# Linear attention and an expert layer on one core: where the routing counts, the turned key table and the first experts' products stand in the attention loop

## The chip, the cores and the metric

The kernel runs on one core of a Trainium2 chip. The metric is the device time of one execution in microseconds, on random inputs of fixed shape. A core has TensorE (PE, with its weight loads PEld), VectorE (DVE), ScalarE (ACT), GpSimd (POOL), and SyncE (SP), which issues most transfers. PE writes to PSUM, of which the kernel uses eight banks of 128 x 512 float32; DVE and ACT read it, POOL does not.

## The reference

Attention with random features for 8 batches of 8 heads, 576 tokens and 64 columns, and then a layer of 8 experts, of which each of the 4608 tokens takes one:

```python
def phi(x):
    proj = np.einsum('bhsd,md->bhsm', x, omega)
    sq = np.sum(x * x, axis=-1, keepdims=True) / 2.0
    h = proj - sq
    h = h - np.max(h, axis=-1, keepdims=True)
    return np.exp(h) / np.sqrt(m)
q_p, k_p = (phi(q_s), phi(k_s))                       # m = 128 features
kv = np.einsum('bhsm,bhsd->bhmd', k_p, v)
z = np.sum(k_p, axis=2)
num = np.einsum('bhsm,bhmd->bhsd', q_p, kv)
den = np.einsum('bhsm,bhm->bhs', q_p, z)[..., None] + 1e-06
...
x = num / den                                         # as (4608, 512)
logits = xn @ en.T / tau                              # of the normalized rows
expert_idx = np.argmax(logits, axis=1)
for e in range(E):
    mask = expert_idx == e
    h = np.maximum(x[mask] @ w1[e], 0.0)              # 512 to 1024 and back
    out[mask] = gate_w[mask, None] * (h @ w2[e])
```

## The kernel before, in words

**The attention loop** has 43 steps, `i` from 0 to 42, over 36 tiles of 128 tokens (4 pairs of batches, 9 tiles each; a batch ends in the middle of the fifth tile of its pair and at the end of the ninth). Steps 0 to 5 have keys only, steps 6 to 35 keys of tile `i` and queries of tile `i - 6`, steps 36 to 41 queries only; the last tile's numerators are in step 42. Keys and queries are projected (`proj`), DVE takes maxima, ACT the exponentials (`feats`). A step later the key features go into the batch's accumulators (`kvmm`, two banks, tags kv0 and kv1), and the query features are transposed into the two banks nu0 and nu1 (`qtr`), copied to SBUF as `qp` (`qcopy`, one half by ACT and one by DVE, in query-only steps both by ACT), and multiplied with the key table into the same two banks (`num`). DVE divides (`num_out`) and writes the token rows `xr` and the experts' logits by head, `lg`, which has one buffer.

**At a batch boundary** (steps 5, 9, 14, 18, 23, 27, 32, 36) ACT empties the accumulators into `kvs`. In the fifth tile of a pair the accumulations for both batches stand in one step. A step later the table is turned by four PE transposes into nu0 (`kv_turn`), DVE copies it out (`kv_turned`), and PE forms the logits' columns of the table behind the numerators (`kv_logits`), which DVE adds to `kvs` (`kv_logits_out`).

**Routing** (`routed`) runs in pieces for each group of three tiles: sum of the logits over heads and their maximum, selection `sel`, counts by PE (a triangular and three full matrices of ones, into nu1), positions, and for each tile an indirect store of its rows by POOL into the buffer `xs`, sorted by expert. Each `next(steps)` does a piece; the dictionaries `spare`, `mid`, `after` and `ends` say at which place of which step. All but the stores and three small copies a group is DVE's or PE's.

**First steps.** After the sixth group the fullest expert so far is picked. Its weights are loaded in steps 27 to 34 and split into high and low halves in steps 29 to 36 by ACT or DVE and POOL (`first_split`). Its first two tiles of rows are computed by `first_steps`, a generator of 38 pieces: two turn a tile of rows, most of the others are three products. A `next(fill)` does one piece. Behind the loop, the remaining pieces stand between the last group's routing, the table of steps that DVE builds, and its transpose `tp`.

**The expert part** then takes 36 steps of 128 rows with three products for one (high and low halves) and streamed weights.

The order on PE and POOL, in the loop also on DVE and ACT, is that of the code; a scheduler orders SP. In the loop of before:

```python
            late = (i,) in mid
            go(spare, i)
            if ts:
                qtr(iq - 1, 1 if late else 0)
            go(mid, i)
            if ts:
                qtr(iq - 1, 0 if late else 1)
            if i >= END - 1:
                next(fill)
```

## Time and profile before

| | |
|---|---|
| time, median of 3 runs | 701.2 us (700.13 to 702.5) |
| profiled execution, its time | 699.2 us |
| profiled execution, its span | 697.5 us |
| PE busy | 654.3 us (94%), 5977 instructions |
| PE weight loads busy | 543.8 us (78%) |
| DVE busy | 567.8 us (81%), 1127 instructions |
| ACT busy | 422.0 us (60%), 1081 instructions |
| POOL busy | 300.4 us (43%), 296 instructions |
| TensorE's granted clock, mean | 0.987 |

The span runs from the first to the last instruction of the profiled execution; the time is that of the whole execution and is a little longer. Busy shares are means over stages with different limits: the attention loop ends at about 249 us, the expert part takes the rest. A granted clock of 1.00 stands for 2.4 GHz, 0.50 for 1.2 GHz.

### The profile page before, as it was taken

The page shows a single profiled execution, that of the slowest core. Times are in us where ns is not written, and L with a number is a line of the kernel's source. Part 1 is how long each engine was busy: PE and PEld are TensorE (multiplying, and loading weights), DVE is VectorE, ACT ScalarE, POOL GpSimd, SP SyncE. Part 2 cuts the span into 40 slices and gives each one's busy share as a digit, 9 for nine tenths or more (in the row PEclk, how much of TensorE's full clock was granted, in tenths as well). Part 3 has the DMA queues.
Part 4 walks back from the last instruction along what each step waited for, and adds up shares of the span by engine and source line. Part 5 has one row for each costly group of instructions (what it writes and reads, how often), then busy time and mean ns, then how long its engine had stood idle before and what let it go on. Part 6 is the DMA issues. An engine that isn't in the chain of part 4 may idle for free. (4 is left out here: it accounts for less than half of the span.)

```text
span 697.5 us, 17954 instructions
## 1 busy us (share of the span) xinstructions
PE 654.3 (94%) x5977; PEld 543.8 (78%) x5978; DVE 567.8 (81%) x1127; ACT 422.0 (60%) x1081; POOL 300.4 (43%) x296
## 2 busy tenths in 40 slices
PE   6899999999796689999999999999999999999994
PEld 6788888888685578778778878788888888878872
DVE  3689899899796652668999999999989998999961
ACT  5798788788786632655374746465555655556430
POOL 2001222113645252444645555464645546463653
PEclk9999999999999979999999999999999999999997
DMA  6445665556942126767787777878688887878620
GB/s 220 142 147 173 181 189 184 185 185 230 333 157 92 63 97 230 237 196 199 209 238 187 223 199 211 200 224 215 199 217 210 224 200 220 200 223 221 178 94 30
DMA packets 142376, 131.85 MB, mean 189 GB/s; under 512 B 106758, under 2 KB 106886, under 8 KB 142288
## 3 DMA queue, kind: packets, MB, share of 16 engines
q1 hardware_dynamic: 135968, 110.30, 57.7%
q0 software_dynamic: 6320, 20.38, 7.7%
q8 instruction: 54, 0.88, 0.5%
q14 instruction: 34, 0.28, 0.1%
HBM read 83.78 MB, written 21.97 MB: 152 GB/s over the span
## 5 line engine op out<-in xcount | busy, mean ns | idle before, releaser
L208 POOL TENSOR_TENSOR w1l<-raww,w1h 128x1024 f32 x34 | 89.3, 2625 | 159.5 <-DVE w1h L207 159.5
L876 DVE COPY wd<-t 128x1024 uint16<-128x1024 uint16 x68 | 116.1, 1710 | 0.5 <-DMA t<-pl 0.5
L242 PE MATMUL nu<-w2h,hh 128*128 (+1 forms) x288 | 114.0, 396 | 0.7 <-POOL w2l L208 0.7
L242 PE MATMUL nu<-w2h,hl 128*128 (+1 forms) x288 | 113.8, 395 | 0.3 <-DVE hl L896 0.3
L242 PE MATMUL nu<-w2l,hh 128*128 (+1 forms) x288 | 113.6, 395 | 0.0
L242 PE MATMUL pa<-w1h,xl 128*128 (+1 forms) x280 | 110.9, 396 | 0.7 <-DVE xl L895 0.7
L242 PE MATMUL pa<-w1h,xh 128*128 (+1 forms) x280 | 110.9, 396 | 0.0
L242 PE MATMUL pa<-w1l,xh 128*128 (+1 forms) x280 | 110.6, 395 | 0.0
L892 ACT ACTIVATE hh<-wd 128x1024 fp32r<-128x1024 f32 x34 | 36.1, 1061 | 119.5 <-DVE wd L876 115.3
L475 POOL DMA_INDIRECT xs<-xr,posi x36 | 35.9, 998 | 138.6 <-DVE nmk L325 34.8
L332 ACT ACTIVATE ftk<-pjk,nmk 128x128 f32<-128x128 f32 x288 | 83.8, 410 | 15.5 <-DVE nmk L325 14.8
L321 PE MATMUL pjk<-om,kt 64*128 64x128 f32 x576 | 80.0, 298 | 6.5 <-DMA kt<-kT 6.3
L208 POOL TENSOR_TENSOR w2l<-raww,w2h 128x1024 f32 x34 | 82.6, 2430 | 0.7
L332 ACT ACTIVATE ftq<-pjq,nmq 128x128 f32<-128x128 f32 x288 | 79.8, 411 | 1.9 <-DVE nmq L325 1.8
L321 PEld LDWEIGHTS pjk<-om,kt 64*128 64x128 f32 x576 | 66.6, 199 | 14.1 <-issue 10.2
L321 PE MATMUL pjq<-om,qt 64*128 64x128 f32 x576 | 76.3, 285 | 0.8 <-ACT ftq L332 0.5
L242 PEld LDWEIGHTS nu<-w2h,hh 128*128 128x128 f32 x288 | 54.2, 188 | 14.0 <-POOL w2l L208 1.4
L321 PEld LDWEIGHTS pjq<-om,qt 64*128 64x128 f32 x576 | 63.6, 187 | 1.5 <-ACT ftq L332 0.7
L242 PEld LDWEIGHTS pa<-w1h,xl 128*128 128x128 f32 x280 | 52.6, 188 | 15.6 <-DVE xl L895 2.5
L242 PEld LDWEIGHTS nu<-w2h,hl 128*128 128x128 f32 x288 | 54.2, 188 | 13.6 <-DVE hl L896 0.7
L242 PEld LDWEIGHTS nu<-w2l,hh 128*128 128x128 f32 x288 | 54.2, 188 | 12.8
L242 PEld LDWEIGHTS pa<-w1l,xh 128*128 128x128 f32 x280 | 52.7, 188 | 12.3
(300 smaller groups left out, 1281.2 us busy)
## 6 DMA issues: line engine op xcount, KB each, us to landing
raww<-w1q SPq DMA_DIRECT2D x38, 512.0 KB, 4.4
raww<-w2q SPq DMA_DIRECT2D x38, 512.0 KB, 5.2
kt<-kT SPq DMA_DIRECT2D x36, 256.0 KB, 3.0
qt<-qT SPq DMA_DIRECT2D x36, 256.0 KB, 3.4
xgp<-xs SPq DMA_DIRECT2D x20, 260.5 KB, 3.1
xg<-xs SPq DMA_DIRECT2D x18, 260.5 KB, 3.1
rf<-w1q SPq DMA_DIRECT2D x4, 512.0 KB, 4.7
rf<-w2q SPq DMA_DIRECT2D x4, 512.0 KB, 5.6
```

The costliest lines, as they stand in the source:

```text
L208: il = nc.gpsimd.tensor_tensor(at(l, dp), raw, at(h, dp).bitcast(F32), op=ALU.subtract)
L242: done.append(nc.tensor.matmul(dst, x[:, c * P : (c + 1) * P], ws.rearrange("p o f -> p (o f)"), start=(begin and i == 0 and k == 0), stop ...
L321: nc.tensor.matmul(st["pj" + w, i, a][:, c, :], st[w, i][r, c, :], om[r, :], start=True, stop=True)
L332: nc.scalar.activation(ft[:, h, :], pj[:, h, :], AF.Exp, bias=nm[:, h : h + 1])
L475: w = nc.gpsimd.indirect_dma_start(out=xs, out_offset=bass.IndirectOffsetOnAxis(ap=posi, axis=0), in_=xr, in_offset=None, bounds_check=ROW ...
L876: nc.vector.tensor_copy(to, src)
L892: nc.scalar.activation(hh, wd[:, 0:F], AF.Relu)
```

## The change

It does six things. The table is turned into a bank with the accumulators' tag kv0. In the fifth tile of a pair the second accumulation stands a step later, for which key features have five buffers and values four (query features two and `qp` two). The counts are two sets of four products on half of the array's columns each, behind the numerators, and the transposes come in the order nu1, nu0. The copy of the turned table stands behind `qcopy`. In eleven of twelve groups the sums over heads and over experts, the masking of positions and their casts are POOL's. And `next(fill)` stands at other places: at the end of steps 37 and 38, behind the maxima in steps 39 to 42, and once more in step 42.

```diff
-                    vt = p1.tile([P, H, D + 1], F32, name=f"vt{i}{key}", tag="vt", bufs=3)
+                    vt = p1.tile([P, H, D + 1], F32, name=f"vt{i}{key}", tag="vt", bufs=4)
...
-            ft = p1.tile([P, 4, M], F32, name=f"ft{which}{i}_{a}", tag=f"ft{which}", bufs=3)
+            ft = p1.tile([P, 4, M], F32, name=f"ft{which}{i}_{a}", tag=f"ft{which}", bufs=5 if which == "k" else 2)
...
-            st["kvtr", sb, b] = tr = nu[0]
+            st["kvtr", sb, b] = tr = ps.tile([P, 512], F32, name=f"kvtr{sb}_{b}", tag="kv0")
...
-            st["qp", i, a] = qp = p1.tile([P, 4, P], F32, name=f"qp{i}_{a}", tag="qp", bufs=4)
+            st["qp", i, a] = qp = p1.tile([P, 4, P], F32, name=f"qp{i}_{a}", tag="qp", bufs=2)
...
         def routed(g):
 
+            eng = nc.gpsimd if g < NTILE // G - 1 else nc.vector
+
+            def total(out, x, axes):
+
+                if eng is nc.vector:
+                    eng.tensor_reduce(out, x.rearrange(axes), axis=AX.X, op=ALU.add)
+                    return
+                for n in (4, 2, 1):
+                    eng.tensor_tensor(x[:, :, 0:n] if n > 1 else out.unsqueeze(2), x[:, :, 0:n], x[:, :, n : 2 * n], op=ALU.add)
+
...
-            nc.vector.tensor_reduce(raw, st["lg", g].rearrange("p g h e -> p g e h"), axis=AX.X, op=ALU.add)
+            total(raw, st["lg", g], "p g h e -> p g e h")
+            if eng is nc.gpsimd:
+                yield
             mx = new("mx", [P, G])
...
-            yield
+            if eng is nc.vector:
+                yield
             sel = sels[g % 2][:, 0:G]
...
-            pr = nu[1][:, P : P + (G + 1) * E].rearrange("p (j e) -> p j e", e=E)
-            nc.tensor.matmul(pr, tri, sels[g % 2], start=True, stop=False)
-            for j in range(G):
-                nc.tensor.matmul(pr[:, j + 1 :], one16, sel[:, j : j + 1].to_broadcast([P, G - j, E]), start=False, stop=j == G - 1)
+            w = 512 - 8 * E
+            pr = nu[1][:, w - (G + 1) * E : w].rearrange("p (j e) -> p j e", e=E)
+            for o in range(0, P, 64):
+                nc.tensor.matmul(pr[o : o + 64], tri[:, o : o + 64], sels[g % 2], start=True, stop=False)
+                for j in range(G):
+                    nc.tensor.matmul(
+                        pr[o : o + 64, j + 1 :], one16[:, o : o + 64], sel[:, j : j + 1].to_broadcast([P, G - j, E]),
+                        start=False, stop=j == G - 1,
+                    )
...
-            nc.vector.tensor_tensor(base, base, sel, op=ALU.mult)
+            eng.tensor_tensor(base, base, sel, op=ALU.mult)
             pos = new("pos", [P, G])
-            nc.vector.tensor_reduce(pos, base, axis=AX.X, op=ALU.add)
+            total(pos, base, "p g e -> p g e")
...
-                nc.vector.tensor_copy(posi, pos[:, j : j + 1])
+                eng.tensor_copy(posi, pos[:, j : j + 1])
...
-            late = (i,) in mid
             go(spare, i)
             if ts:
-                qtr(iq - 1, 1 if late else 0)
-            go(mid, i)
-            if ts:
-                qtr(iq - 1, 0 if late else 1)
-            if i >= END - 1:
+                qtr(iq - 1, 1)
+                qtr(iq - 1, 0)
+            if i == END:
                 next(fill)
...
                 qcopy(iq - 1, 0, not ks)
+            go(mid, i)
...
-            if i == END:
+            if i > NTILE + 2:
                 next(fill)
...
-                for b in range(2 if u == 4 else 1):
+                for j, b in ([(i - 2, 1)] if u == 5 else []) + [(i - 1, int(u > 4))]:
                     for a in range(2):
-                        kvmm(i - 1, a, b or int(u > 4))
+                        kvmm(j, a, b)
...
+            if NTILE < i <= NTILE + 2:
+                next(fill)
...
-                for d, key in ((ends, i + 1), (spare, i + 2), (spare, i + 2), (ends, i + 2), (ends, i + 3), (ends, i + 4)):
+                for d, key in ((ends, i + 1), (after, i + 2), (ends, i + 2), (ends, i + 2), (ends, i + 3), (ends, i + 4)):
```

What stands in a row on DVE at step 10, behind the batch boundary of step 9 and the first group's end (`kvc` is the table to be turned, `kvts` its turned copy, `nmk` and `nmq` are maxima, `raw` the summed logits). Before:

```order
L358 COPY kvc_1_874<-kvs_1_843 128x2x4x64
L441 TENSOR_REDUCE raw_876<-lg_636 128x24
L443 TENSOR_REDUCE mx_878<-raw_876 128x3
L444 TENSOR_TENSOR raw_876<-raw_876,mx_878 128x24
L371 COPY kvts_1_908<-nu_70 128x512
L325 TENSOR_REDUCE nmk_1_914<-pjk_1_890 128x4
L399 COPY qp_0_928<-nu_70 128x512
L325 TENSOR_REDUCE nmq_0_935<-pjq_0_891 128x4
```

With the change, at the same place:

```order
L358 COPY kvc_1_875<-kvs_1_844 128x2x4x64
L325 TENSOR_REDUCE nmk_1_910<-pjk_1_887 128x4
L399 COPY qp_0_924<-nu_70 128x512
L371 COPY kvts_1_926<-kvtr_1_897 128x512
L325 TENSOR_REDUCE nmq_0_933<-pjq_0_888 128x4
L325 TENSOR_REDUCE nmq_1_959<-pjq_1_913 128x4
```

The three routing operations have left this place, and the copy of the turned table has moved from ahead of the maxima to behind `qp`.

On PE, steps 41 and 42 before (`fs_x` is a tile of the first expert's rows, turned; `fs_a` the first steps' product), from the last count to the second piece behind `num` of step 42:

```order
L457 MATMUL nu_71<-sel_125,one_77 128x8
L391 MATMUL nu_70<-ident,ftq_0_4630 128x128 x4
L391 MATMUL nu_71<-ident,ftq_1_4664 128x128 x4
L228 MATMUL fs_x_4705<-ident,xgp_105 128x128 x4
L410 MATMUL nu_70<-kvs_1_4316,qp_0_4717 64x73 x8
L410 MATMUL nu_71<-kvs_1_4316,qp_1_4715 64x73 x8
L391 MATMUL nu_70<-ident,ftq_0_4719 128x128 x4
L391 MATMUL nu_71<-ident,ftq_1_4752 128x128 x4
L228 MATMUL fs_x_4774<-ident,xgp_106 128x128 x4
L242 MATMUL fs_a_4803<-w1h 128x512
L242 MATMUL fs_a_4803<-w1l,w1h 128x512
L242 MATMUL fs_a_4803<-w1h 128x512
```

With the change, step 42 on PE:

```order
L391 MATMUL nu_71<-ident,ftq_1_4879 128x128 x4
L391 MATMUL nu_70<-ident,ftq_0_4835 128x128 x4
L242 MATMUL fs_a_4687<-w1h 128x512
L242 MATMUL fs_a_4687<-w1l,w1h 128x512
L242 MATMUL fs_a_4687<-w1h 128x512
L242 MATMUL fs_a_4915<-w1h 128x512
L242 MATMUL fs_a_4915<-w1l,w1h 128x512
L242 MATMUL fs_a_4915<-w1h 128x512
L410 MATMUL nu_70<-kvs_1_4395,qp_0_4910 64x73 x8
L410 MATMUL nu_71<-kvs_1_4395,qp_1_4908 64x73 x8
```

The tiles' turning and the first three pieces of products have gone to steps 37 to 41, and step 42 has the fourth and the fifth piece between the transposes and the numerators.

On POOL, steps 39 and 40 with the change: the end of the square root for the first steps' norms (`rt_p`), the row number and the second store of the tenth group (`posi`), and the sum over heads of the eleventh (`lg`, `raw`):

```order
L132 TENSOR_TENSOR rt_p<-rtt_p,rt_p 128x2
L133 TENSOR_TENSOR rt_p<-rt_p,n2p 128x2
L418 COPY xr_4707<-ids 128x1
L491 CAST posi_4722<-pos_4628 128x1
L493 DMA xs<-xr_4300,posi_4722 38016x576
L445 TENSOR_TENSOR lg_4503<-lg_4503 128x3x32
L445 TENSOR_TENSOR lg_4503<-lg_4503 128x3x16
L445 TENSOR_TENSOR raw_4727<-lg_4503 128x24
L418 COPY xr_4781<-ids 128x1
```

Before, the square root's last operation stood behind all but two of the eleventh group's stores, and no sum was on POOL.

## Rows read from the trace of the kernel before

**Rows 1.** Busy time by stretch. Columns: the stretch (us from the span's start) and its length, then busy us of each engine with its count of instructions, TensorE's granted clock (1.00 is 2.4 GHz), the mean busy share of the DMA engines, GB/s. The cuts are the first numerator product (L410) of step 7, the one of step 36, the one of step 42, the first product of the expert part's loop, and 680.
```profile
33.30:211.30 178.00, 167.22 (x3256) 149.33 (x3254) 157.06 (x495) 146.85 (x511) 50.31 (x103) 1.00 0.61 195
211.30:248.80 37.50, 25.50 (x393) 21.54 (x393) 22.72 (x86) 21.87 (x68) 13.00 (x28) 0.91 0.21 71
248.80:276.80 28.00, 27.19 (x151) 22.25 (x152) 12.71 (x75) 5.84 (x13) 11.53 (x26) 0.93 0.49 162
276.80:680.00 403.20, 401.50 (x1741) 322.69 (x1740) 357.48 (x428) 226.65 (x420) 214.76 (x106) 1.00 0.77 206
```

**Rows 2.** PE's waits in the stretch 33.3 to 211.3 us: waiting tile and line, the engine, tile and line that ended the wait, us in total, times, longest.
```profile
PE nu L391 <- DVE kvts L371: 3.7, 6, 1.9
PE nu L455 <- DVE sel L451: 2.2, 9, 0.5
PE nu L410 <- DVE qp L399: 1.5, 2, 0.9
```

**Rows 3.** Order of time in step 19, behind a batch boundary: PE, then DVE. Columns of this and the following rows in order of time: start us, us, engine, line, operation, out<-in, tile size, shape, count, and in brackets the idle time before it and what ended that.
```profile
100.96 0.66 PE L367 MATMUL nu<-ident,kvc 128*128 128x128 f32 x4
101.46 0.60 PE L391 MATMUL nu<-ident,ftq 128*128 128x128 f32 x4
102.41 0.66 PE L391 MATMUL nu<-ident,ftq 128*128 128x128 f32 x4 [0.36 <-DVE kvts L371]
...
101.67 0.68 DVE L371 COPY kvts<-nu 128x512 f32<-128x512 f32 x1
```

**Rows 4.** Order of time on PE in step 23: the counts of one group and the first transposes behind them.
```profile
124.61 0.18 PE L455 MATMUL nu<-sel,tri 128*128 128x32 bf16 x1 [0.19 <-DVE sel L451]
124.63 0.22 PE L457 MATMUL nu<-sel,one 128*128 128x24 bf16 x3
124.71 0.52 PE L391 MATMUL nu<-ident,ftq 128*128 128x128 f32 x3
```

**Rows 5.** Order of time on PE, 211 to 252 us, the numerator products alone: steps 36 to 42.
```profile
211.27 1.25 PE L410 MATMUL nu<-kvs,qp 128*64 128x73 f32 x32 [1.41 <-ACT qp L397]
...
217.96 1.25 PE L410 MATMUL nu<-kvs,qp 128*64 128x73 f32 x32 [0.69 <-ACT qp L397]
...
224.47 1.25 PE L410 MATMUL nu<-kvs,qp 128*64 128x73 f32 x32 [1.18 <-ACT qp L397]
...
229.14 1.25 PE L410 MATMUL nu<-kvs,qp 128*64 128x73 f32 x32 [1.18 <-ACT qp L397]
...
233.80 1.25 PE L410 MATMUL nu<-kvs,qp 128*64 128x73 f32 x32 [1.18 <-ACT qp L397]
...
241.28 1.28 PE L410 MATMUL nu<-kvs,qp 128*64 128x73 f32 x32 [2.27 <-ACT qp L397]
...
248.77 2.21 PE L410 MATMUL nu<-kvs,qp 128*64 128x73 f32 x32 [0.99 <-ACT qp L397]
```

**Rows 6.** Busy time by stretch in the query-only steps (columns as in rows 1), and ScalarE's eviction for the first steps' tile in step 41, in order of time.
```profile
236.00:242.00 6.00, 2.66 (x42) 2.17 (x40) 3.25 (x12) 2.96 (x9) 1.18 (x2) 1.00 0.13 47
242.00:252.00 10.00, 7.86 (x68) 6.55 (x63) 3.21 (x15) 3.46 (x10) 3.61 (x15) 0.52 0.07 28
...
239.04 0.60 ACT L229 ACTIVATE w1h<-fs_x 128x512 fp32r<-128x512 f32 x1 [3.24 <-PE fs_x L228]
```

**Rows 7.** Order of time on PE in step 5: the second accumulation at the first batch boundary.
```profile
23.59 0.63 PE L347 MATMUL kva<-vt4v,ftk 128*64 128x65 f32 x14 [1.09 <-ACT kvs L354]
```

**Rows 8.** Order of time in steps 32 and 33: PE, then DVE.
```profile
184.35 2.28 PE L347 MATMUL kva<-vt31v,ftk 128*64 128x65 f32 x64
...
187.19 0.49 PE L321 MATMUL pjk<-om,kt 64*128 64x128 f32 x2 [0.56 <-DMA kt<-kT]
...
191.96 0.44 PE L391 MATMUL nu<-ident,ftq 128*128 128x128 f32 x2 [1.91 <-DVE kvts L371]
...
191.21 0.69 DVE L371 COPY kvts<-nu 128x512 f32<-128x512 f32 x1 [3.69 <-POOL w2l L514]
```

**Rows 9.** GpSimd's groups of instructions by line and shape, 100 to 211 us: line, engine, operation, out<-in, shapes, count, then busy us and mean ns of one, idle time before and what ended most of it.
```profile
L514 POOL TENSOR_TENSOR w1l<-rf,w1h 128x256 fp32r<-128x256 f32 x13 | 9.1, 738 | 0.1
...
L446 POOL COPY xr<-raw 128x8 f32<-128x8 f32 x18 | 2.7, 193 | 0.0
```

**Rows 10.** Order of time in steps 33 and 34: GpSimd, then DVE.
```profile
198.72 2.78 POOL L514 TENSOR_TENSOR w1l<-rf,w1h 128x256 fp32r<-128x256 f32 x4
...
201.31 0.19 DVE L426 TENSOR_TENSOR lg<-nu,rr 128x32 f32<-128x32 f32 x1
```

**Rows 11.** Order of time behind the last step: DVE, PE, ScalarE.
```profile
251.83 0.17 DVE L256 TENSOR_SCALAR rt_p<-rt_p 128x2 f32<-128x2 f32 x1 [1.54 <-POOL rt_p L133]
...
252.12 0.14 DVE L423 TENSOR_SCALAR rr<-nu 128x4 f32<-128x4 f32 x1
...
255.21 0.18 PE L455 MATMUL nu<-sel,tri 128*128 128x32 bf16 x1 [0.50 <-DVE sel L451]
...
265.07 0.27 PE L787 MATMUL tp<-ident,tab 128*5 128x128 f32 x1
...
276.76 0.39 PE L242 MATMUL pa<-w1h 128*128 128x512 f32 x1
...
277.91 1.06 ACT L203 ACTIVATE w1h<-raww 128x1024 fp32r<-128x1024 f32 x1 [8.44 <-DMA raww<-w1q]
```

**Rows 12.** One line's instructions in the whole span: count, then shortest, median and longest ns of one, first and last start, form.
```profile
L444 DVE TENSOR_TENSOR raw<-raw,mx x12: 182/182/641, 47.7 to 254.3; 128x24 f32<-128x24 f32 x12
```

## Prediction

> **What bounds the kernel now.** I read the page's forty slices first, to see where TensorE (PE) is not full, then busy time by stretch, then PE's waits in each stretch, then the single steps in order of time. [Rows 1] cut the span at the products `num` of step 7, of step 36 and of step 42, and at the first product of the expert part. From 276.8 us on PE is busy 401.50 of 403.20 us: the expert part is bound by PE and nothing in the change touches it, so whatever is gained ahead of it should stay gained. Ahead of it PE is idle 10.8 us in the 178.0 us of the steps with keys and queries, 12.0 us in the 37.5 us of the query-only steps, and 0.8 us in the 28.0 us behind them. So at most some 23 us lie there, plus what PE loses to its clock.
>
> In the steps with keys and queries PE is the bound (94% busy), VectorE (DVE) is next (157.06 of 178.00). PE's waits there with a name [rows 2]: the query transposes for the turned key table's copy, 3.7 us in 6 waits; the counts for `sel`, 2.2 us in 9; the numerators for DVE's copy `qp`, 1.5 us in 2. [Rows 3] show the first kind: `kv_turn` writes nu0 at 100.96, the transposes of nu1 follow at 101.46, those of nu0 stand until DVE has copied the table out (101.67 plus 0.68).
>
> The query-only steps are bound by a chain, not by an engine: numerators, DVE's division, transposes, ScalarE's copies `qp`, numerators again. [Rows 5] have the starts of `num` in steps 36 to 42, so six intervals: 6.69, 6.51, 4.67, 4.66, 7.48, 7.49 us, and ahead of each PE waits for ACT's `qp`. 4.66 is the bare chain. In the last two the first steps' tile turning stands in the chain: ACT evicts it from 239.04 on, ahead of the `qp` copies, and `num` at 241.28 waits 2.27 us for those [rows 5, 6]. PE was busy 2.66 of 6.00 us before 242, and then its granted clock is 0.52 over ten microseconds, which is nearly all at the lower of its two levels: `num` of step 42 takes 2.21 us for 1.25 [rows 5, 6].
>
> **The change, part by part.** The sum is of differences against the profiled execution.
>
> *Key-only steps.* The second accumulation at a batch boundary moves one step later. In step 5 it waited 1.09 us for ACT to empty its bank [rows 7]. Its 32 products keep their price. Between 0 (ACT's exponentials then set the pace) and -1.09 I take the middle: **-0.5**.
>
> *Steps with keys and queries.* The turned table gets the accumulators' bank, which is empty by then, so the transposes of nu0 no longer wait: -3.7. DVE's copy comes behind `qp`; what needs it is the table's logits, behind a projection group and the numerators, and the next accumulation in that bank, later still. The counts come behind the numerators, half a step after `sel` is ready: -2.2. Of the 1.5 us for DVE's `qp`, one wait has the logits' sum on DVE ahead of it, which goes to GpSimd (POOL): -0.5. Given back: (a) the counts are eight products of half width for four. Four of full width span 0.24 us, and the transposes start 0.10 us after them [rows 4]; eight lie between 0.10 and 0.48. They now hold the division in nu1 and, with the reading of their sums, the transposes of nu1, but PE's own work behind them is as much later. I take 0.15, so +0.05 for each of 9 groups: +0.5 (bounds 0, +3.4). (b) In step 32, 64 products of the two accumulations take 2.28 us, and then PE still waits 0.56 us for the key tile [rows 8]. With 32 of them moved out, PE arrives 1.1 us earlier at a load that comes no earlier, and does the 32 in step 33: +1.1 (bounds 0, +1.1). (c) POOL. No row has its sums; the nearest are 0.193 us for 128x8 and 0.738 us for 128x256 [rows 9]. The three adds of a group have 96, 48 and 24 elements a partition: bounds 0.6 and 2.2 us, 0.9 taken, being nearer the small one. `lg` has one buffer, so DVE's next group may not write it until the adds are done. Most of a step lies between, and the shortest takes 4.66 us [rows 5], except where POOL splits first weights: at step 33 it splits from 198.72 for 2.78 us, the adds would end at 202.4, and DVE writes `lg` at 201.31 [rows 10]: +1.1 (bounds 0, +2.4). Another wait on such a split falls out of the path: the table's copy stood until 191.21 for POOL, and PE with it 1.91 us, inside the 3.7 above [rows 8]. Sum: **-3.7**. DVE's loss of the sums and casts counts nothing here, since PE covers it; were DVE the bound it would be a gain.
>
> *Query-only steps.* After the change I make the intervals so. Steps 36 to 37: the 0.69 us wait for `qp` shrinks, as its transposes wait no more for the table: 6.1. 37 to 38: the counts and the five short DVE operations ahead of them leave the chain, the turning of the first tile comes in, 0.60 us on ACT and as much on DVE ahead of the table's logits: 5.75. 38 to 39: the bare 4.66, the counts 0.15 and DVE's reading of their sums, two short operations of 0.18 [rows 12], and DVE's part of the second turning, put at ACT's 0.60: 5.75. 39 to 40: 4.66; the piece of three products lies in PE's 1.18 us wait. 40 to 41: 4.66, plus 0.3, since POOL's square root (13 operations) now stands ahead of the sum that frees `lg`: 5.0. 41 to 42: 4.66, counts and reading 0.5, the exponentials on ACT ahead of `qp`, put at one eviction's 0.60: 5.75. Sum 33.0 for 37.5: **-4.5** (bounds -7 if the chain is bare, 0 if each piece lengthens it). This takes PE at the full clock: by [rows 1] it has two thirds of its time busy in the stretch and falls only behind the 44% of [rows 6], and the new pieces fill it to some 75%.
>
> *Behind the last step.* From `num` at 248.77 DVE reaches its second division at 252.12, having waited 1.54 us for POOL's square root, PE at the lower clock meanwhile [rows 5, 11]. With the root three steps earlier this is about the 1.3 us of a full-clock `num`: **-2.1** (bounds 0, -2.2).
>
> *Pieces done earlier.* Seven calls of `fill` stand in the loop for three: four pieces of three products. Fourteen pieces still stand between the last counts and the table's transpose, 255.21 to 265.07, so 0.70 us each [rows 11]; that distance stays. Behind it, up to 276.76, four pieces are missing: -2.8. The weights of the second expert come no earlier than the table, and ACT waits for them at 277.91 [rows 11], ahead of evictions that PE needs soon: bounds 0 and -2.8, **-2.0** taken.
>
> Sum: -0.5 -3.7 -4.5 -2.1 -2.0 = -12.8, so a span of 684.7 and 686.4 us for the profiled run of 699.2. That run is 2.0 us under the median of the runs shown, 701.2; on it the forecast is 688.4.
>
> **A rule against the change.** One DVE form shows a disturbance: `raw` minus its maximum takes 0.182 us at the median of 12 but 0.641 once [rows 12]. The Trainium skill, "SBUF — State Buffer", section "SBUF: two separate sides", says that VectorE and GpSimd share one pair of ports as an exclusive lock, so that an operation of one that needs it blocks the other for its whole length. By that rule ten new POOL operations a group would stop DVE's two-input operations; the row does not say what stood on POOL, and its median is undisturbed. The sum takes nothing for it; if each of the 11 groups cost the 0.46 us of the one long row, the time would be 5.1 us more.
>
> **The rivals.**
> 1. *GpSimd late, slower.* Place: DVE's first write of `lg` and its reading of `raw`. For: [rows 10] show POOL late once by itself. Against: elsewhere most of a step is free, and the dear bound for the three adds is 2.2. It decides once the adds outlast that gap by more than 1.2 us a group; at 1.5 us the 11 groups stop DVE for 16.5, and the time is 705. Chance 0.07, a third of it near no change.
> 2. *The waits only move.* DVE is 88% busy; with the division held by the counts, and the second transpose group now that of nu0, PE may wait for DVE elsewhere by as much as it no longer waits [rows 1, 2]. Then -3.7 falls away: 692.1. Chance 0.17.
> 3. *The clock falls all the same* in the last query-only steps: the pieces run at half speed inside the chain. -4.5 shrinks to -1 and -2.1 to -0.5: 693.5. Chance 0.12.
> 4. *DVE stopped by POOL* at the two-input operations, 0.46 us a group: 693.5. Chance 0.06.
> 5. *All idle time of the double steps goes.* The 10.8 us of [rows 1] less some 1.3 us for the key tile (0.56 and more, given back (b)), and the 2.8 whole: 701.2 - 0.5 - 9.5 - 4.5 - 2.1 - 2.8 = 681.8. Chance 0.13.
>
> The forecast itself has 0.45, with a range of its own of 685.5 to 691.5.
>
> **How the numbers follow.** Predicted is the likeliest case, 688.4. The range goes from 683.5, inside rival 5, to 694.5, beyond rivals 2 to 4; rival 1 and the far half of rival 5 are left out. A measurement of this kernel tells about 0.3%, 2.1 us, from no change. All cases but rival 1 are faster by more: 0.93; no change 0.02; slower 0.05.
>
> **What would show each step right or wrong.** PE's list of waits without the table's copy and without `sel`; the counts next to the numerators, eight of them, and the division of nu1 behind them. Intervals of `num` in the query-only steps near 5 to 6 us and a granted clock of 1.00 there. The second division of step 42 about 1.3 us behind `num`. From the table's transpose to the first expert product 9 us for 11.7. The stretch of the expert part unchanged at about 403 us. Wrong would be: new DVE waits for POOL at `lg` outside the split steps, PE waits for the division ahead of the transposes, or a clock of 0.5 in the query-only steps.

## The result, and the profile after

The changed kernel takes 690.2 us (median of 4 runs, 689.5 to 690.5), the kernel before beside it 701.0; the ratio is 0.984 [0.982, 0.986]. Two later sets of runs, on two different chips, gave the same kernel 686.9 and 686.4 us, ratios 0.979 [0.976, 0.983] and 0.979 [0.976, 0.982]. All lie in the range, on the forecast's side of no change. The sum of the forecast, 12.8 us, stands beside 10.8, 13.6 and 14.0. How it came about is another matter: of its five terms only the two behind the loop hold, as a sum, in all three profiles.

Busy time by stretch of the changed kernel, with the cuts of [rows 1] (columns as there), first in its first profile (whose span is 688.6 us), then in a second one of the same kernel (684.6 us):

```profile
30.92:208.75 177.83, 166.72 (x3290) 150.71 (x3288) 148.72 (x444) 149.15 (x509) 70.33 (x190) 1.00 0.60 193
208.75:244.71 35.96, 27.58 (x411) 23.43 (x411) 21.50 (x78) 23.43 (x73) 22.42 (x63) 0.95 0.22 76
244.71:268.65 23.94, 22.90 (x143) 18.67 (x143) 12.15 (x69) 4.74 (x8) 8.71 (x15) 1.00 0.52 171
```
```profile
31.86:206.00 174.14, 165.06 (x3291) 149.80 (x3289) 148.23 (x444) 149.15 (x509) 70.30 (x190) 1.00 0.61 197
206.00:241.26 35.26, 26.96 (x411) 22.58 (x411) 21.54 (x78) 23.20 (x73) 21.72 (x63) 0.97 0.21 71
241.26:264.88 23.62, 23.39 (x143) 19.21 (x143) 12.15 (x69) 4.74 (x8) 9.33 (x15) 0.97 0.54 186
```

Each stretch's gain on the profile before, in us (negative is shorter; the second and third profile are of the same changed kernel, taken with the later sets; the last column is the changed kernel with all routing sums on DVE, below):

| stretch | before | forecast | first profile | second | third | sums on DVE |
|---|---|---|---|---|---|---|
| to `num` of step 7 | 33.3 | -0.5 | -2.4 | -1.4 | -2.1 | -2.1 |
| keys and queries | 178.0 | -3.7 | -0.2 | -3.9 | -3.9 | -7.1 |
| query-only | 37.5 | -4.5 | -1.5 | -2.2 | -0.3 | -5.0 |
| step 42 to first expert product | 28.0 | -4.1 | -4.1 | -4.4 | -4.9 | -4.7 |
| from there to the end | 420.7 | 0 | -0.8 | -1.0 | -0.7 | -0.5 |

PE's waits in the steps with keys and queries, in the first profile (columns as in [rows 2]). The table's copy and `sel` have left the place they had there; what has come is short waits for many things:

```profile
PE pjk L321 <- ACT ftq L332: 1.7, 2, 1.3
PE kvtr L367 <- DVE kvc L358: 1.7, 4, 0.5
PE nu L391 <- DVE mx L455: 1.6, 2, 0.9
PE nu L410 <- DVE qp L399: 1.5, 2, 1.0
PE nu L378 <- DVE kvts L371: 1.0, 1, 1.0
PE kva L347 <- issue: 0.8, 2, 0.4
```

The third kind goes back to GpSimd. In order of time around step 31: POOL splits a first weight, then sums the eighth group, and DVE's first write of `lg` in the next group stands until that is done, so that `mx`, for which PE waits, comes late. The same wait of DVE is in steps 34 and 37, behind splits too, and in step 40, behind GpSimd's square root (columns as in [rows 3]):

```profile
173.18 2.78 POOL L532 TENSOR_TENSOR w2l<-rf,w2h 128x256 fp32r<-128x256 f32 x4
175.93 0.74 POOL L445 TENSOR_TENSOR lg<-lg 128x96 f32<-128x96 f32 x2
176.75 0.24 POOL L445 TENSOR_TENSOR raw<-lg 128x24 f32<-128x24 f32 x1
...
177.02 0.19 DVE L426 TENSOR_TENSOR lg<-nu,rr 128x32 f32<-128x32 f32 x1 [1.95 <-POOL raw L445]
...
199.15 0.19 DVE L426 TENSOR_TENSOR lg<-nu,rr 128x32 f32<-128x32 f32 x1 [1.16 <-POOL raw L445]
...
218.06 0.19 DVE L426 TENSOR_TENSOR lg<-nu,rr 128x32 f32<-128x32 f32 x1 [0.75 <-POOL raw L445]
...
234.53 0.19 DVE L426 TENSOR_TENSOR lg<-nu,rr 128x32 f32<-128x32 f32 x1 [0.34 <-POOL raw L445]
```

The forecast had one such wait, of 1.1 us, in step 34, from [rows 10].

### The profile page after: what moved, and what is told of

Its sections match the earlier page's. It is cut to its first block, busy times and chain, and to the rows that moved or that the text cites. A ratio compares the mean times of both kernels' runs of the same rounds, so it can differ in the third digit from the quotient of the medians.

```text
span 688.6 us, 18006 instructions
## 1 busy us (share of the span) xinstructions
PE 650.1 (94%) x6025; PEld 542.4 (79%) x6026; DVE 557.9 (81%) x1061; ACT 425.5 (62%) x1081; POOL 327.0 (47%) x406
## 5 line engine op out<-in xcount | busy, mean ns | idle before, releaser
L321 PE MATMUL pjk<-om,kt 64*128 64x128 f32 x576 | 78.5, 292 | 7.2 <-DMA kt<-kT 5.4
L242 PEld LDWEIGHTS nu<-w2h,hl 128*128 128x128 f32 x288 | 54.1, 188 | 13.6 <-DVE hl L914 0.6
L242 PEld LDWEIGHTS nu<-w2l,hh 128*128 128x128 f32 x288 | 54.1, 188 | 12.8
L242 PEld LDWEIGHTS pa<-w1h,xh 128*128 128x128 f32 x280 | 52.6, 188 | 12.0
```

The lines of the kernel that those rows point to most:

```text
L242: done.append(nc.tensor.matmul(dst, x[:, c * P : (c + 1) * P], ws.rearrange("p o f -> p (o f)"), start=(begin and i == 0 and k == 0), stop ...
L321: nc.tensor.matmul(st["pj" + w, i, a][:, c, :], st[w, i][r, c, :], om[r, :], start=True, stop=True)
```

## The experiments

Times stand against the kernel before in the same set of runs; runs of one set share a chip. The first set holds the second profile, two buffers, sums on DVE and the old places of the pieces; the second the third profile and three parts undone or alone; the third the last four.

**The same kernel again, twice.** No edit.

> The changed kernel itself, unaltered, for a second profile. Two readings of the first profile are open. Chance: numerators of step 7 started 2.4 us earlier than before, of which 0.7 us was there already at the first transfers, and TensorE stood three times 0.4 to 0.7 us inside accumulations with nothing named that it waited for; if these are chance, the second profile has the first numerators 0.5 us or more off 30.9, and the stalls in other steps or none. Cause in the program: the same 30.9 within 0.2 and stalls in the same three steps. Time 690.2 by both.

> The changed kernel itself a third time, beside the three other runs of this call. The two profiles so far differ by 4.0 us of span, of which 3.7 lie in the steps with keys and queries: in the first TensorE stood in steps 13, 18 and 21 inside accumulations with no named wait. Theory E, these stalls are chance of an execution: a third profile has them in other steps or not at all, and its stretch from the numerators of step 7 to those of step 36 is either near 174 (none) or up to 178 (some). Theory F, they are the program's and the second profile was the exception: stalls in the same three steps, near 178.

Measured 686.9 and 686.4 us. The stretch with keys and queries takes 174.14 and 174.15 us: 3.7 less than in the first profile. Step by step (a step's length is the time from its `num` to the next) 2.7 of them lie in steps 13 (0.5), 18 (1.2) and 21 (1.0), and 0.9 in five others. In the first profile PE, DVE and POOL stand like this in step 18:

```profile
95.42 1.06 PE L347 MATMUL kva<-vt17v,ftk 128*64 128x65 f32 x27
96.89 0.35 PE L347 MATMUL kva<-vt17v,ftk 128*64 128x65 f32 x5 [0.41 <-issue]
...
97.01 0.16 DVE L423 TENSOR_SCALAR rr<-nu 128x4 f32<-128x4 f32 x1 [1.10 <-PE kva L347]
...
95.53 0.98 POOL L493 DMA_INDIRECT xs<-xr,posi  x1 [0.28 <-POOL posi L491]
```

PE stops inside an accumulation, and DVE's second reading of numerators waits with it. Neither expectation holds whole: the second and third profile have no such stop, but a profile of another kernel below has them in the same steps 13, 18 and 21. So they are neither scattered nor the program's alone. The chip is an open rival: the undisturbed profiles with sums on GpSimd are from two chips, the disturbed one below is from a third, and that of the first profile is not on record. In these steps a store of POOL begins 0.5 to 1.2 us behind the start of `num`; before it was 3.5 us or more. But the undisturbed profiles have the stores at the same distance there (1.18 us in steps 18 and 21). What sets them off stays open. That they account for the 3 us between the first times and the later ones is argued from profiles, not shown; that all four times beside the first profile (689.5 to 690.5) lie above all eight of the later ones (684.0 to 687.8) speaks for something that lasts through a set of runs.

**Two buffers for `lg`.**

```diff
-  st["lg", g] = small.tile([P, G, H, E], F32, name=f"lg{g}", tag="lg", bufs=1)
+  st["lg", g] = small.tile([P, G, H, E], F32, name=f"lg{g}", tag="lg", bufs=2)
...
```

> The changed kernel with two buffers for the logits by head (room is made by letting the small table tiles behind the loop share one of them). In the changed kernel VectorE waited four times for GpSimd's sums of the group before (1.95, 1.16, 0.75, 0.34 us), since the one buffer was still being read. Theory A, GpSimd's late sums took the gain of the steps with keys and queries: the four waits go, the stretch from the numerators of step 7 to those of step 36 falls from 177.8 to about 175.3, the query-only steps by about 1, time about 686.7. Theory B, VectorE is the next bound and the waits only move: the stretch stays within 0.8 of 177.8, time about 689.5.

Measured 684.7 us, 0.976 [0.974, 0.978]. That is 2.2 less than the changed kernel beside it; theory A had 3.5 less, B 0.7. A holds in the waits: all four are gone (0.9 us has come at `mx`), and the intervals of `num` at steps 31, 34, 37 and 40 shrink from 7.14, 6.83, 6.51 and 5.40 (second profile) to 6.25, 5.69, 5.80 and 4.65, together 3.5 us. But step 32 takes 12.7 us for 8.7. SP's issues ahead of it, PE in it, and the stretch cut at the end of the wait (for the columns see [rows 1]):

```profile
170.81 0.34 SPq L521 DMA_DIRECT2D rf<-w2q  x1
171.42 0.34 SPq L521 DMA_DIRECT2D rf<-w1q  x1
172.63 0.33 SPq L521 DMA_DIRECT2D rf<-w2q  x1
173.07 0.64 SPq L297 DMA_DIRECT2D kt<-kT  x1
...
182.51 0.76 PE L321 MATMUL pjk<-om,kt 64*128 64x128 f32 x2 [4.18 <-DMA kt<-kT]
...
175.97:182.50 6.53, 2.35 (x72) 2.23 (x73) 4.31 (x14) 4.56 (x17) 4.89 (x11) 0.85 1.01 379
182.50:188.66 6.16, 6.15 (x44) 5.62 (x45) 1.68 (x3) 1.63 (x5) 4.10 (x8) 0.61 0.46 141
```

Three first weights of 512 KB are issued ahead of the key tile, the DMA engines are full until it lands 9.3 us after its issue, and behind PE's 4.2 us of standing still the granted clock is 0.61, partly at the lower level. In the kernel before the three loads stand ahead of it too, and it lands 8.2 us after its issue. TensorE comes 1.5 us earlier than in the second profile, to a tile that lands 0.6 us later. Over all profiles of this study the key or query tile held TensorE there for 0 to 4.2 us, and the step took 6.4 to 13.2 us; so a difference of a microsecond or two in steps 31 to 33 of one profile says little of a change.

**All sums on VectorE.**

```diff
-            eng = nc.gpsimd if g < NTILE // G - 1 else nc.vector
+            eng = nc.vector
```

> The changed kernel with all sums, masks and casts of the routing back on VectorE (as in the last group), everything else as changed. Theory A (the late GpSimd sums cost some 3.4 us in the steps with keys and queries): that stretch falls by 1 to 2 us, since VectorE has time for them, time about 688.5. Theory B (VectorE is the next bound): VectorE has about 9 us more work in that stretch, and the transposes wait for it 0.3 us or more a group: the stretch grows by 3, time about 693.5. In the query-only steps the sums stand in the chain by both: up to 1 us more, less the 1.1 us of waits for GpSimd.

Measured 681.1 us, 0.972 [0.970, 0.974]: 5.9 us under the changed kernel beside it, better than theory A. Steps 10 to 29 are within 0.15 us of the second profile each (but 0.3 at steps 14 and 23); the gain lies in steps 30 to 35 and in the query-only steps:

```profile
31.24:202.14 170.90, 164.15 (x3291) 149.44 (x3289) 155.70 (x496) 147.72 (x509) 49.83 (x103) 1.00 0.62 201
202.14:234.65 32.51, 25.98 (x411) 22.04 (x411) 22.84 (x88) 22.64 (x71) 15.85 (x40) 1.00 0.21 75
```

PE's named waits in the first stretch are now 6.4 us, none of them for the routing. DVE does 7.5 us more there, and the stretch is shorter all the same. The query-only intervals are 6.03, 5.87, 5.66, 4.65, 4.66, 5.64. The forecast had 6.1, 5.75, 5.75, 4.66, 5.0, 5.75.

One thing else differs. At the end of step 30 DVE's copy of a first weight, from SBUF to SBUF, starts while GpSimd still splits, and both are held up. In the second profile of the changed kernel, and then with all sums on DVE, where the split is done first:

```profile
165.64 2.78 POOL L532 TENSOR_TENSOR w1l<-rf,w1h 128x256 fp32r<-128x256 f32 x4
168.38 0.64 POOL L418 COPY xr<-ids 128x1 int32<-128x1 int32 x1
...
167.84 1.14 DVE L529 CAST w2h<-rf 128x1024 fp32r<-128x1024 f32 x1
```
```profile
164.48 2.80 POOL L532 TENSOR_TENSOR w1l<-rf,w1h 128x256 fp32r<-128x256 f32 x4
167.22 0.18 POOL L418 COPY xr<-ids 128x1 int32<-128x1 int32 x1
...
167.39 0.68 DVE L529 CAST w2h<-rf 128x1024 fp32r<-128x1024 f32 x1
```

DVE loses 0.46 us there, and so does GpSimd, which goes on from there to the late sum of the eighth group; the same happens in step 36. What part of the 5.9 us this makes is not shown.

**The pieces at their old places.** Three `next(fill)` in the loop: in steps 41 and 42 behind the transposes, in step 42 behind the maxima.

```diff
-            if i == END:
+            if i >= END - 1:
                 next(fill)
...
-            if i > NTILE + 2:
+            if i == END:
                 next(fill)
...
-            if NTILE < i <= NTILE + 2:
-                next(fill)
```

> The changed kernel with the pieces of the first steps at their places of before (three in the loop for seven), everything else as changed. Theory C, as the prediction has it: the pieces' place made the gains behind the last step and most of those in the last two query-only steps; without it numerators of step 42 to the first expert product take about 28 again for 23.9, the last two intervals 7.5 each for 5.4 and 7.25, less some 1.4 that the pieces cost in steps 37 to 39: time about 695.2. Theory D, TensorE's work is only moved, and what is not done in the loop is done behind it in the same time: the query-only steps lose 2.5 us of work and the part behind gains it: time about 691.0.

Measured 693.4 us, 0.989 [0.987, 0.991], 6.5 us over the changed kernel beside it; theory C had 5.0 over the 690.2, D 0.8. C is nearer and D falls: in the profile it is 27.9 us behind step 42 for 23.6, and the query-only steps take 37.9 for 35.3, the last two 6.7 and 9.1 where C had 7.5 each. (Another 1.9 us lie in the steps with keys and queries, which the pieces don't touch; it is the slowest execution of the four.) Step 41 has the lower clock again:

```profile
235.75:244.86 9.11, 5.83 (x55) 5.24 (x56) 2.99 (x13) 4.21 (x13) 2.44 (x8) 0.63 0.08 29
```

**The table and the accumulation of the fifth tile as before.**

```diff
-            st["kvtr", sb, b] = tr = ps.tile([P, 512], F32, name=f"kvtr{sb}_{b}", tag="kv0")
+            st["kvtr", sb, b] = tr = nu[0]
...
                 qtr(iq - 1, 1)
+            go(mid, i)
+            if ts:
                 qtr(iq - 1, 0)
...
                 qcopy(iq - 1, 0, not ks)
-            go(mid, i)
...
-                for j, b in ([(i - 2, 1)] if u == 5 else []) + [(i - 1, int(u > 4))]:
+                for b in range(2 if u == 4 else 1):
                     for a in range(2):
-                        kvmm(j, a, b)
+                        kvmm(i - 1, a, b or int(u > 4))
```

> The changed kernel with two of its parts undone: the turned table goes into nu0 again, copied out between the two groups of transposes, and both accumulations of a pair's fifth tile stand in one step again. Theory G, the terms of the prediction: 3.7 us of waits for the table's copy come back and 1.1 for the key tile goes, key-only steps lose 0.5, so 3 us more than the changed kernel beside it. Theory H, these two parts were worth more than their named waits: step 5 loses some 1.5, and behind each of the other seven boundaries 0.5 instead of the 0.36 named, 2.1 at the split in step 32: 5.5 us more or above. Rival I, the waits for the table were replaced by others (for the copy of the table before it is turned, for VectorE's copy ahead of the logits): less than 1 us more.

Measured 690.6 us, 0.986 [0.984, 0.989], 4.2 over the changed kernel: between G and H, rival I falls. `num` of step 7 starts 2.1 us later; five boundaries cost 0.3 to 0.4 us each, steps 32 to 34 2.5.

**The counts as before.** Four products on the whole array ahead of the transposes, with their reading; order nu0, nu1.

```diff
...
+                qtr(iq - 1, 0)
                 qtr(iq - 1, 1)
-                qtr(iq - 1, 0)
...
-                for d, key in ((ends, i + 1), (after, i + 2), (ends, i + 2), (ends, i + 2), (ends, i + 3), (ends, i + 4)):
+                for d, key in ((ends, i + 1), (spare, i + 2), (spare, i + 2), (ends, i + 2), (ends, i + 3), (ends, i + 4)):
```

> The changed kernel with the counts ahead of the transposes again, as four products on the whole array, in the order nu0, nu1 as before; all else as changed. Theory J, the term of the prediction (2.2 us of waits for the selection, less 0.5 for the halves): the stretch with keys and queries grows by 1.7, and the query-only steps by up to 1, as the selection stands in the chain: 2 to 3 us more than the changed kernel beside it. Rival K, the counts behind the numerators hold the second division and with it the transposes by as much (in the changed kernel each step with counts is 0.3 us over the bare 5.31, in the query-only steps 1.0 over 4.66): no difference, within 1 us.

Measured 692.9 us, 0.991 [0.987, 0.994], 6.6 over the changed kernel, more than either theory. It is no clean test: with the sums a piece of their own on GpSimd, the maximum and the selection are one row of five DVE operations in the step ahead, and the counts wait up to 1.6 us for it, 9.4 in ten waits; and PE waits 3.1 us for a key tile. The two parts lean on each other, so the counts were tried alone on the kernel before (below).

**The later accumulation alone, on the kernel before.** The change of `kvmm` above and its buffers.

> The kernel before with one part of the change alone: the second accumulation of a pair's fifth tile a step later, with the numbers of buffers that go with it (key features five, query features two, values four, qp two). Theory G (the prediction): step 5 gains 0.5, the later boundaries nothing, since in step 32 TensorE only comes earlier to a key tile that is not there: 0.5 to 0.6 us less than before, 700.0. Theory H: the numerators of step 7 come 1.5 us earlier, and some more at the later pairs: 698.5 or below. Rival: the smaller numbers of buffers for query features and their copies hold ScalarE: no gain, 700.6 or above.

Measured 702.4 us beside 700.3, 1.0019 [1.0003, 1.0034]: no gain, and if anything a loss, within 0.3%. From the first product of step 4's accumulation to `num` of step 7 it takes 10.46 us; the kernel before takes 11.95, as do the two others here without the later accumulation (11.88 and 11.95), and the ten profiles with it and the new bank take 10.29 or 10.30. So H is right on step 5. Each of the two pairs at steps 14 and 23 gives back 0.25, and steps 32 and 33 2.5: PE comes early and stands 3.1 us for the table's copy, which waits 3.7 for POOL's split, as in [rows 8]. Another 1.4 us go in step 38, at a granted clock of 0.72, and 1.3 in the expert part, which it doesn't touch. The rival has the time right, but of its cause the trace shows one wait of ScalarE, 1.1 us for the accumulation of a key tile. With the table's new bank PE no longer waits for that copy ahead of the transposes; that this part then pays is argued from the profiles, as no run has these two parts alone.

**The counts alone, on the kernel before.** The new matrices, places and the order nu1, nu0.

> The kernel before with one part of the change alone: the counts behind the numerators as two sets of four on half of the array's columns, the transposes always in the order nu1, nu0. Theory J, the prediction's term: 2.2 us of waits for the selection go and 0.5 comes back in the steps with keys and queries, 1.7 less; with up to 1 in the query-only steps 698 to 699. Theory O, the term was too small, since the old counts also stood 0.24 us ahead of the transposes themselves: 0.3 to 0.4 us a group, 3 us in all: 697.0. Rival K, the second division held by the counts gives all back: 700.4 within 0.6.

Measured 695.5 us, 0.993 [0.991, 0.995]: 5.2 less, theory O and beyond. Each group gains 0.6 us where `sel` and the counts stood ahead of the transposes, and loses 0.2 a step later: 0.41 to 0.46 for six of the seven groups up to step 29. The stretch falls by 1.4 in the profiled execution, by 4.0 without steps 32 and 33 (there 2.6 us are lost: PE waits 0.7 us for a key tile and 0.9 for nothing named, and the clock is 0.59 behind that; it is the slowest execution of nine, 699.0).

**GpSimd's sums for seven groups alone.**

```diff
-            eng = nc.gpsimd if g < NTILE // G - 1 else nc.vector
+            eng = nc.gpsimd if g < 7 else nc.vector
```

> The changed kernel with the routing sums on GpSimd for the first seven groups alone; from the eighth on, where GpSimd also splits first weights and the query-only steps come, they are VectorE's. All sums on VectorE gave 681.1. Theory L, GpSimd's sums cost only where they queue behind splits or stand in the query-only chain: 681.1 within 0.8, and steps 10 to 29 like the changed kernel's. Theory M, GpSimd's operations stop VectorE's wherever they meet: seven groups at the 0.46 us of the one long row, some 3 us more than with all on VectorE: 684. Theory N, the sums off VectorE help it while the steps are full: 680 or below.

Measured 687.3 us, 0.982 [0.979, 0.984]. No theory gave that. Steps 33 to 41 are those with all sums on DVE, to 0.05 us, as L says; steps 10 to 29 those of the second profile, except the stops of the first profile in steps 13, 18 and 21, 3.6 us with their followers; and step 32 takes 11.3 us (PE waits 1.5 for ACT, 1.7 for a query tile, then a clock of 0.67). So in steps 10 to 29 the sums on GpSimd cost nothing but the stops, whose cause is open; the two kernels below, from the same set and with all sums on DVE, have none.

M, that GpSimd stops DVE wherever they meet, falls in that form by DVE's own rows. Three of DVE's groups, first with the sums on GpSimd (second profile), then on DVE: a two-input operation with one input in PSUM, the copy from SBUF to SBUF, and a two-input operation on SBUF alone:

```profile
L430 DVE TENSOR_TENSOR xr<-nu,rr 128x256 f32<-128x256 f32 x58 | 24.3, 419 | 0.0
L529 DVE CAST w2h<-rf 128x1024 fp32r<-128x1024 f32 x3 | 2.6, 858 | 0.0
L464 DVE TENSOR_TENSOR sel<-iotm,mx 128x24 bf16<-128x24 f32 x9 | 1.9, 209 | 0.3
```
```profile
L430 DVE TENSOR_TENSOR xr<-nu,rr 128x256 f32<-128x256 f32 x58 | 24.2, 418 | 0.0
L529 DVE CAST w2h<-rf 128x1024 fp32r<-128x1024 f32 x3 | 2.1, 684 | 0.0
L464 DVE TENSOR_TENSOR sel<-iotm,mx 128x24 bf16<-128x24 f32 x9 | 1.6, 183 | 0.3
```

The first is not stopped. The copy is, by 0.17 us on the mean of three, and `sel` by 0.03 us.

**The transposes in the order nu0, nu1,** with all sums on VectorE; first in the query-only steps, then in all.

The edit of the first:

```diff
...
-                qtr(iq - 1, 1)
-                qtr(iq - 1, 0)
+                for a in (1, 0) if ks else (0, 1):
+                    qtr(iq - 1, a)
...
-                qcopy(iq - 1, 1, True)
-                qcopy(iq - 1, 0, not ks)
+                for a in (1, 0) if ks else (0, 1):
+                    qcopy(iq - 1, a, a == 1 or not ks)
```

> All sums on VectorE as in the run that gave 681.1, and in the query-only steps the order nu0, nu1 for the transposes and ScalarE's copies. Theory P: there VectorE reads nu0 0.6 us before it is done with nu1, so the transposes that now wait for the last reader of nu1 (0.5 to 1.9 us a step) can begin with nu0: the intervals of the numerators fall by 0.4 to 0.5 us each in five of six steps (32.5 together to about 30.2), time about 678.8. Theory Q: the transposes of nu1 and ScalarE's second copy end no earlier, since both hang on the same last reader, and the intervals stay: 681.

> As the last, with the order nu0, nu1 in the steps with keys and queries too (there ScalarE still copies nu1 and VectorE nu0). Theory P: the reader of nu1 (counts, logits of the table) has 0.5 us more, VectorE's copy of nu0 comes 0.5 us earlier and the waits of the numerators for it (1.8 us) go: the stretch from the numerators of step 7 to those of step 36 falls from 170.9 by 1 to 2 us, time about 677.3. Theory Q: ScalarE's copy of nu1 comes 0.5 us later and holds the numerators: no gain over the last or up to 2 us slower.

Measured 678.1 us, 0.969 [0.966, 0.972], and 677.5, 0.968 [0.965, 0.970]. The query-only intervals fall from 32.5 to 30.9 together: P, at two thirds of its size. (The times are 3.0 and 3.6 us under the 681.1, but that is from another set.) PE in step 42, first with nu1 ahead, then with nu0:

```profile
232.26 1.06 PE L391 MATMUL nu<-ident,ftq 128*128 128x128 f32 x8 [1.88 <-DVE base L481]
```
```profile
229.65 0.52 PE L391 MATMUL nu<-ident,ftq 128*128 128x128 f32 x3 [1.21 <-DVE xr L430]
```

The transposes no longer stand behind DVE's reading of the counts. In the steps with keys and queries the order is worth 0.3 us for P's 1 to 2, which the times don't tell apart. These are the fastest kernels here, 3% under the kernel before.

## Why the prediction was right, point by point

**In total** it was right with errors that cancel, and in so far by luck: gains and losses were both put too small. Of the signs that it named for being wrong, one came (a wait at `lg` in step 40, where nothing is split and the sum had 0.3 us) and one in part (the lower clock, in step 41).

**Key-only steps, -0.5.** Mis-sized: 1.66 us by the 11.95 and 10.29 above, outside the bounds. With the bank's 1.09 us [rows 7] went a wait of PE for `ftq`, 0.55, and 0.70 of its busy time (10.31 to 9.61 in the third profile), as the projections of keys and queries behind it now run side by side; 0.68 came back as a wait for `kvc`. The forecast priced one wait and held the rest of the chain fixed. The rest of the column, -0.7 to +0.2, goes with PE's wait for the second key tile: 0.57 us before, 0.85 in the second profile, none in the others.

**Keys and queries, -3.7.** The sum was right in two of three profiles (-3.9), its parts were not. The counts were worth 4.0 alone for a forecast of 1.7, since [rows 2] show the wait for `sel` but not the counts' own time ahead of the transposes. The table's bank took its 3.7 us of waits away, but 2.7 stand in the first profile for `kvc` and at the table's logits, where 0.3 did. The 0.5 at `qp` did not come: 1.5 us of these waits before, 1.5 after. "Given back (c)", POOL, is the term that failed: 3.2 us net for 1.1 (174.15 less 170.90). The price of three adds was right, 0.98 us [0.74 and 0.24 above] for 0.9. What failed is the place: the forecast looked for splits where [rows 10] had one, but the kernel splits in each of steps 29 to 36, and in two of them (30 and 33) a sum queued behind a split, with PE's transposes behind DVE. "Given back (b)", the key tile, was bounded by 1.1; waits go to 4.2 us, and behind the longest the clock was 0.61.

**Query-only steps, -4.5.** The intervals were right to 0.35 us each, for a kernel whose sums are DVE's. With them on POOL each sum waits in the chain (intervals at steps 36, 37, 40: +0.4, +0.6, +0.7), which the forecast left out: it counted `lg` in the shortest step only. The largest miss is the last interval, put at 5.75 with PE at the full clock: 7.25, 6.62 and 7.26 us in the three profiles, at a granted clock of 0.76, 0.83 and 0.76, and 5.64 at 1.00 with the sums on DVE. The forecast's argument from PE's share of busy time did not hold: in the second profile PE was busy 4.10 of 5.40 us in step 40 and 2.48 of the next 4.36, and then the clock was 0.51 to the end of step 41. In the third the clock falls in step 38 too (0.77). So rival 3 came true in part. Step 41 of the first profile:

```profile
237.46:244.71 7.25, 5.36 (x54) 4.55 (x54) 2.67 (x14) 4.49 (x15) 3.12 (x9) 0.76 0.09 37
```

**Behind the last step, -2.1, and pieces done earlier, -2.0.** Right as a sum: -4.1 to -4.9 together, and undoing the pieces' places alone brings 4.2 us back. The second division begins 2.14, 1.85 and 1.29 us behind `num` in the three profiles for 3.35, so only the third has the whole -2.1. From the table's transpose to the first expert product it is 9.23 us for 11.69 in each, -2.5 for -2.0; ahead of it 0.4 us went that the forecast held fixed.

**The rivals.** 1 (GpSimd late) was a true mechanism at a third of its price, at four of the eleven groups' ends. 2 (the waits only move) is what the first profile looks like by its length, but 3.6 us of that are the stops and their followers, and the next two profiles do not have them. 4 (DVE stopped by POOL, the Trainium skill's "SBUF — State Buffer", section "SBUF: two separate sides") is seen, below its price: operations with an input in PSUM are not touched (419 against 418 ns), those on SBUF alone are. In the second profile three of these (`w2h`, `kvc`, `sel`) take 1.6 us more of DVE's time in all than with the sums on DVE, for the rival's 5.1. The one long `raw` of [rows 12] stands beside a store of GpSimd, and has a like (632 ns) in the kernel without GpSimd's sums. 5 (681.8) has the time of the kernel without GpSimd's sums, 681.1, by chance: its stretch with keys and queries gave 7.1 us, not 9.5. The Trainium skill, "Perfetto Trace Analysis", section "Optimizing GPSIMD Operations", advises to prefer other engines where possible; this case agrees, at 5.9 us. What it shows is in the main a queue: a second buffer for `lg` alone takes 3.5 us from the four steps with waits, which shrink by 4.7 with all sums on DVE.

## What to carry to other kernels

Before small work goes to an idle engine, list what stands in its queue at each place where the work will stand, and ask who waits for the result: a low share of busy time (28% of that stretch before, by [rows 1]) is no answer when 2.8 us of splitting stand ahead of 1 us that a chain needs. A part can shorten the stage that it is in and lose it again at a wait further on (the later accumulation alone), so parts are tried both alone and undone. In a chain through two buffers, try to refill first the one whose last reader is done first; here that was worth 1.6 us in six steps.

## What the runs showed of the hardware

- PE can stop with nothing named: in the same three steps in two profiles, which are 0.5 to 1.2 us longer for it, and not in five other profiles of kernels with a store as near behind `num`; in the profile of the counts alone at three other places, 0.35 to 0.94 us. The cause stays open.
- A key tile of 256 KB issued behind three transfers of 512 KB landed 9.3 us later, with the DMA engines' share at 1.01, and PE's standing still was followed by a clock of 0.61.
- DVE's operations with an input in PSUM took the same time with 87 more POOL operations in the stretch (190 for 103). A copy of DVE from SBUF to SBUF that began during a split of GpSimd took 1.14 us for 0.68, and GpSimd's short copy behind that split 0.64 for 0.18.
